# Weight slices of 512 columns for features 4 to 11, and an earlier issue for features 2 and 3, in an attention and feed-forward kernel

## Chip, cores and metric

One core of one Trainium2 chip. The time is the device time of one execution in microseconds (us), as the median of several executions; executions of one kernel mostly agree within about 1 us here. A profiled execution gives the trace from which all durations are read.

## What is computed

Linear attention followed by a gated feed-forward block, on 8,192 tokens (8 batches of 1,024) with 512 channels and 1,536 hidden columns:

```
k_proj, v_proj = E @ k, F @ v                 # per batch and head, 1024 rows -> 64
x      = softmax(q @ k_proj^T / 8) @ v_proj   # 8 heads of 64
g      = x @ w_gate ;  val = x @ w_val        # 512 x 1536 each
out    = (g * sigmoid(g) * val) @ w_out       # 1536 x 512
```

Inputs and weights are float32 in HBM. GpSimd's DMAs convert what they load to bf16 on the way in.

## The kernel before

The 1,536 hidden columns are 12 *features* of 128 columns. Tokens come in 16 chunks of 512. For every chunk and feature TensorE runs four matmuls for the gate and four for the value. The gate and value weights are loaded once, during the first 40 us, in slices of columns, and each slice is one DMA with one completion. All loads below are issued by GpSimd, in program order, between its normalisations (`u_N`).

```python
    def load_w_gv(c0, c1, which=(0, 1)):          # features c0 to c1-1; gate, then value
        cs = slice(c0 * P, c1 * P)
        for wsrc, wdst in [((moe_w_gate, wg), (moe_w_val, wv))[i] for i in which]:
            nc.gpsimd.dma_start(
                out=wdst[:, :, cs],
                in_=wsrc[:, cs].rearrange("(t p) c -> p t c", p=P),
            )
    ...
        load_q(0, 0, (0, 2))
        load_k(0, 4, 8)
        load_q(0, 0, (2, 4))
        load_v(0, (0, 4, 6, 8))
        load_w_gv(0, 1)
        load_w_gv(1, 2, (0,))
        ...
        u_N(0, 0)                                 # the first normalised unit
        load_w_gv(1, 2, (1,))
        ...
        u_N(0, 2)
        ...
        u_N(0, 1)
        load_w_gv(2, 4)
        ...
        load_w_gv(4, 6)
        load_q(0, 1)
        for f in (6, 8, 10):
            load_w_gv(f, f + 2)
        load_wo(0); load_wo(1); load_k(1)
        ...                                       # then chunk after chunk:
            f_g(c, f, i)                          # four gate matmuls, tanh on ScalarE
            run_slot(2 * t)                       # transposes of the next chunk's q, ...
            f_v(c, f, i)                          # four value matmuls, products on VectorE
```

The softmax here doesn't subtract the row's maximum and nothing guards it: scores larger than these inputs give would overflow.

## Time and profile before

| | before |
|---|---|
| time at the prediction | 573.21 us (573.05 to 573.64, 3 runs) |
| span of the profiled execution | 571.7 us |
| TensorE busy | 564.2 us |
| waits of TensorE for wg or wv | feature 6: 0.61 us (gate) + 0.29 us (value) |
| everything after feature 4 of the second chunk | 516.1 us |

"Busy" is time in which an engine executes; TensorE's 99% leaves little to win anywhere. Its timeline is the view that counts: in the columns start, duration, engine, line, operation, count, a bracket tells how long the engine was idle before and who ended it. The lines of before are in the prediction.

### The profile page before, as it was taken

Reading aid. Unit: us, or ns where it says so; the run is one execution under the profiler, and the core shown is the slowest. Engines: PE = TensorE matmul, PEld = TensorE weight load, DVE = VectorE, ACT = ScalarE, POOL = GpSimd, SP = SyncE. Lnnn points to the kernel's source line nnn. Section 1 sums busy time; section 2 is a strip of 40 time slices with the busy share of each in tenths; the row PEclk is TensorE's granted clock in tenths of the full one; section 3 lists DMA queues with packets and bytes.
Section 4 is the critical chain, followed back from the end, with each engine's and each line's share of the span. In section 5 each row is a group of like instructions: output and inputs, shape, how many; then the busy total and the mean of one; then the engine's idle time right before and its main releaser. Section 6 shows DMA issues by size and latency. Waiting matters only on the chain.

```text
span 571.7 us, 7944 instructions
## 1 busy us (share of the span) xinstructions
PE 564.2 (99%) x2971; PEld 268.5 (47%) x2971; DVE 336.6 (59%) x581; ACT 238.3 (42%) x421; POOL 109.2 (19%) x122
## 2 busy tenths in 40 slices
PE   8999999999999999999999999999999999999997
PEld 4644444444444444444444444444444444444444
DVE  3677566666466654666556665567546674554540
ACT  3555434354435434444335434354342543443232
POOL 6834121134002500124001330023200220000000
PEclk9999999999999999999999999999999999999999
DMA  9999993549901697038940499204990124100012
GB/s 202 176 199 206 202 177 77 89 71 197 202 29 47 113 192 148 19 75 129 196 100 37 64 176 196 63 20 90 196 176 37 44 50 75 38 37 23 33 38 92
DMA packets 106983, 61.86 MB, mean 108 GB/s; under 512 B 60096, under 2 KB 98240, under 8 KB 106944
## 3 DMA queue, kind: packets, MB, share of 16 engines
q0 software_dynamic: 42800, 29.36, 35.7%
q1 hardware_dynamic: 63232, 30.42, 24.7%
q10 hardware_dynamic: 912, 1.57, 1.0%
q8 instruction: 23, 0.38, 0.3%
q14 instruction: 16, 0.13, 0.1%
HBM read 60.29 MB, written 16.78 MB: 135 GB/s over the span
## 4 chain that ended last, share of the span: by engine, by line
PE 92%; DMA 3%; DVE 2%; POOL 1%; ACT 1%; issue 0%; DVEq 0%; POOLq 0%
PE yps L362 29%; PE vps L324 27%; PE gps L324 27%; PE kvp L149 3%; PE sc L229 2%; PE pv L287 2%; DMA wv<-in_moe_w_val_dram 2%; DMA qb<-in_q_dram 1%; DVE zz L244 1%; POOL AA L260 0%; POOL wg L117 0%; PE qTp L195 0%; DVE hT L348 0%; ACT xT L137 0%; DVE s L343 0%
## 5 line engine op out<-in xcount | busy, mean ns | idle before, releaser
L343 DVE SCALAR_TENSOR_TENSOR s<-th,gps 128x512 f32<-128x512 f32 x192 | 130.5, 680 | 139.2 <-ACT th L336 138.8
L324 PE MATMUL gps<-xT,wg 128*128 128x512 bf16 (+1 forms) x776 | 197.8, 377 | 0.7 <-DMA wg<-in_moe_w_gate_dram 0.4
L324 PE MATMUL vps<-xT,wv 128*128 128x512 bf16 (+1 forms) x776 | 197.5, 377 | 0.1
L362 PE MATMUL yps<-wo,hT 128*128 128x512 bf16 (+1 forms) x780 | 194.5, 376 | 0.0
L336 ACT ACTIVATE th<-gps 128x512 f32<-128x512 f32 x192 | 114.6, 597 | 163.4 <-PE gps L324 161.9
L348 DVE TENSOR_TENSOR hT<-s,vps 128x512 bf16<-128x512 f32 x192 | 132.0, 687 | 22.1 <-PE vps L324 1.5
L362 PEld LDWEIGHTS <-hT 128*128 128x128 bf16 x780 | 76.2, 98 | 89.9
L260 POOL TENSOR_TENSOR AAd<-ee,rr 128x512 bf16<-128x512 f32 x52 | 54.1, 1040 | 319.5 <-issue 178.1
L324 PEld LDWEIGHTS <-wv 128*128 128x128 bf16 x776 | 73.8, 98 | 83.2 <-issue 3.3
L324 PEld LDWEIGHTS <-wg 128*128 128x128 bf16 x776 | 74.0, 98 | 81.9 <-DMA wg<-in_moe_w_gate_dram 0.9
L372 ACT ACTIVATE ysb<-yps 128x512 f32<-128x512 f32 (+1 forms) x65 | 38.4, 590 | 78.1 <-PE yps L362 78.1
L137 ACT CAST xT<-pv 128x512 bf16<-128x512 f32 x63 | 36.7, 584 | 51.2 <-PE pv L287 50.3
L244 DVE TENSOR_REDUCE zz<-ee 128x8 f32<-128x512 f32 x64 | 43.5, 679 | 19.4 <-ACT ee L233 19.4
L233 ACT ACTIVATE ee<-sc 128x512 f32<-128x512 f32 x64 | 37.9, 596 | 18.0 <-PE sc L229 17.9
L287 PE MATMUL pv<-AT,BDV 128*128 128x512 bf16 x60 | 22.6, 379 | 0.0
L229 PEld LDWEIGHTS <-qTd 128*128 128x128 bf16 x208 | 16.0, 98 | 12.3
L229 PE MATMUL sc<-BD,qTd 128*128 128x128 bf16 x208 | 20.1, 219 | 0.0
L137 DVE CAST BDV<-kvp 64x256 bf16<-64x256 f32 x14 | 6.0, 427 | 22.1 <-ACT ks L159 19.1
L260 POOL TENSOR_TENSOR AA<-ee,rr 128x512 bf16<-128x512 f32 x11 | 11.4, 1038 | 36.3 <-DVE rr L246 34.4
L246 DVE RECIPROCAL rr<-zz 128x8 f32<-128x8 f32 x64 | 13.0, 203 | 6.7 <-DVE zz L244 0.5
L149 PE MATMUL kvp<-vb,FT 128*64 128x512 bf16 (+2 forms) x80 | 15.7, 339 | 0.3 <-ACT BDV L137 0.3
L149 PE MATMUL kvp<-kb,ET 128*64 128x512 bf16 (+1 forms) x72 | 15.5, 358 | 0.3 <-DVE kb L137 0.2
(51 smaller groups left out, 146.4 us busy)
## 6 DMA issues: line engine op xcount, KB each, us to landing
out_dram<-ysb SPq DMA_DIRECT2D x63, 256.0 KB, 2.4
qb<-in_q_dram POOLq DMA_DIRECT2D x15, 512.0 KB, 16.9
kb<-in_k_dram POOLq DMA_DIRECT2D x7, 1024.0 KB, 11.3
vb<-in_v_dram POOLq DMA_DIRECT2D x7, 1024.0 KB, 14.0
wo<-in_moe_w_out_dram POOLq DMA_DIRECT2D x2, 768.0 KB, 15.3
wg<-in_moe_w_gate_dram POOLq DMA_DIRECT2D x5, 256.0 KB, 9.6
wv<-in_moe_w_val_dram POOLq DMA_DIRECT2D x5, 256.0 KB, 10.2
kraw<-in_k_dram ACTq DMA_DIRECT2D x2, 512.0 KB, 5.0
```

The source lines that it names most:

```text
L137: (nc.scalar.copy if eng is nc.scalar else eng.tensor_copy)(out=out, in_=in_)
L149: nc.tensor.matmul(out=t[lo : lo + 64, h0:h1].rearrange("p h d -> p (h d)"), lhsT=w[:, j, :], rhs=src[b][:, h0:h1, j, :], start=(j == 0), ...
L229: nc.tensor.matmul(out=ps[:, n, :], lhsT=t[:, n, :], rhs=BD[b % 2][:, 4 * g + n, :], start=True, stop=True)
L233: nc.scalar.activation(out=e[:].rearrange("p h j k -> p (h j k)"), in_=ps[:].rearrange("p a k -> p (a k)"), func=AF.Exp, scale=scale,)
L244: nc.vector.reduce_sum(out=z[:], in_=e[:], axis=AX.X)
L260: eng.tensor_tensor(out=a.rearrange("p j h k -> p h j k"), in0=ee.pop((b, u))[:], in1=rr.pop((b, u))[:].unsqueeze(3).to_broadcast([P, 4, 2 ...
L324: nc.tensor.matmul(out=ps[:, ts], lhsT=(wg, wv)[w][:, kt, f * P : (f + 1) * P], rhs=x[:, kt, ts], start=(kt == 0), stop=(kt == NKT - 1),)
L336: nc.scalar.activation(out=th[:], in_=ps[:], func=AF.Tanh, scale=0.5)
L343: nc.vector.scalar_tensor_tensor(out=s1[:], in0=th[:], scalar=1.0, in1=g[:], op0=ALU.add, op1=ALU.mult)
L348: nc.vector.tensor_tensor(out=hT[c][:, f, :], in0=s1[:], in1=ps[:], op=ALU.mult)
L362: nc.tensor.matmul(out=yy[c][:, cs], lhsT=hT[c][:, f, i * P : (i + 1) * P], rhs=wo[:, f, cs], start=(f == 0), stop=(f == NFT - 1),)
L372: nc.scalar.activation(out=ysb[:, cs], in_=yy[c][:, cs], func=AF.Copy, scale=0.5)
```

## The change

Intent: use an idle stretch of GpSimd for the transfers of features 2 and 3, and move later weights in fewer, wider slices.

```diff
         u_N(0, 0)
         load_w_gv(1, 2, (1,))
+        load_w_gv(2, 4)
         ...
         u_N(0, 1)
-        load_w_gv(2, 4)
         ...
-        load_w_gv(4, 6)
+        load_w_gv(4, 8)
         load_q(0, 1)
-        for f in (6, 8, 10):
-            load_w_gv(f, f + 2)
+        load_w_gv(8, 12)
```

## The prediction

> **What bounds the kernel now.** I read the page first, then the waits of TensorE, then its timeline around the longest real wait, then GpSimd's timeline and the DMA issues one at a time.
>
> ```profile
> span 571.7 us, 7944 instructions
> PE 564.2 (99%) x2971; PEld 268.5 (47%) x2971; DVE 336.6 (59%) x581; ACT 238.3 (42%) x421; POOL 109.2 (19%) x122
> ...
> PE 92%; DMA 3%; DVE 2%; POOL 1%; ACT 1%; issue 0%; DVEq 0%; POOLq 0%
> PE yps L362 29%; PE vps L324 27%; PE gps L324 27%; PE kvp L149 3%; PE sc L229 2%; PE pv L287 2%; DMA wv<-in_moe_w_val_dram 2%; DMA qb<-in_q_dram 1%; DVE zz L244 1%; POOL AA L260 0%; POOL wg L117 0%; PE qTp L195 0%; DVE hT L348 0%; ACT xT L137 0%; DVE s L343 0%
> ```
>
> The first two lines cap everything: TensorE is busy 564.2 of 571.7 us, so a change that leaves its instructions alone has 7.5 us to play with, start and end of the program included. The chain says where a load still counts: its only weight entry is one transfer of wv, 2% of the span (10.19 us at 23.88 in time order). That is a path, not a gain; the gain is the idle time at its end. The timeline of TensorE there (start, duration, engine, line, operation, count, idle before and who ended it):
>
> ```profile
> 28.68 1.03 PE L324 MATMUL gps<-xT,wg 128*128 128x512 bf16 x4
> 29.55 1.03 PE L324 MATMUL vps<-xT,wv 128*128 128x512 bf16 x4
> 30.41 1.03 PE L324 MATMUL gps<-xT,wg 128*128 128x512 bf16 x4
> 31.27 1.03 PE L324 MATMUL vps<-xT,wv 128*128 128x512 bf16 x4
> 32.74 1.04 PE L324 MATMUL gps<-xT,wg 128*128 128x512 bf16 x4 [0.44 <-DMA wg<-in_moe_w_gate_dram]
> 33.61 0.39 PE L195 MATMUL qTp<-ident_bf,qb 128*128 128x128 bf16 x4
> 34.12 1.04 PE L324 MATMUL vps<-xT,wv 128*128 128x512 bf16 x4
> ```
>
> Groups of four follow each other every 0.86 us. Counting features from the head, 28.68 is feature 4 (gate), 29.55 its value, 30.41 and 31.27 feature 5, 32.74 and 34.12 feature 6. Feature 6 should have begun at 31.27 + 0.86 = 32.13: it is 0.61 late. Its value group should have followed at 32.74 + 0.87 + 0.22 (the four transposes) = 33.83: 0.29 late. Together 0.90 us of waiting for weights, and I find no other wait of this size for wg or wv anywhere in the run.
>
> GpSimd issues these loads, in its order:
>
> ```profile
> 13.59 1.04 POOL L260 TENSOR_TENSOR AA<-ee,rr 128x512 bf16<-128x512 f32 x1 [2.69 <-DVE rr L246]
> 14.58 0.80 POOL L117 DMA_DIRECT2D wv<-in_moe_w_val_dram  x1
> 17.28 2.04 POOL L260 TENSOR_TENSOR AA<-ee,rr 128x512 bf16<-128x512 f32 x2 [1.89 <-ACT ee L233]
> 19.27 0.80 POOL L117 DMA_DIRECT2D wg<-in_moe_w_gate_dram  x1
> 20.07 0.75 POOL L117 DMA_DIRECT2D wv<-in_moe_w_val_dram  x1
> ```
>
> It idles 1.89 us from 15.38 to 17.28, behind two normalisations that wait for ScalarE and VectorE, and only then issues features 2 and 3. Asked one by one, the issues land at (issue start + time to landing): value of feature 1, 14.58 + 8.0 = 22.6; gate 2-3, 19.27 + 4.7 = 23.9; value 2-3, 20.07 + 5.2 = 25.3; gate 4-5, 20.80 + 6.4 = 27.2; value 4-5, 21.53 + 7.0 = 28.5; q, 22.27 + 9.1 = 31.4; gate 6-7, 23.14 + 9.55 = 32.7; value 6-7, 23.88 + 10.19 = 34.1. The last two are exactly the two late groups. So until 34 us the weights are in a race with TensorE, and the queue is never empty. What it moves, by stretch (busy time of PE, PEld, DVE, ACT, POOL; clock, DMA share, GB/s):
>
> ```profile
> 21.00:22.00 1.00, 1.00 (x13) 0.88 (x11) 0.78 (x2) 0.28 (x1) 1.00 (x2) 1.00 1.34 131
> 22.00:23.00 1.00, 1.00 (x11) 0.90 (x10) 0.25 (x1) 0.58 (x1) 1.00 (x2) 1.00 1.34 170
> 23.00:24.00 1.00, 1.00 (x12) 0.89 (x10) 0.00 (x0) 0.14 (x1) 1.00 (x3) 1.00 1.46 191
> 24.00:25.00 1.00, 1.00 (x11) 0.88 (x9) 0.51 (x1) 0.72 (x2) 1.00 (x2) 1.00 1.15 128
> ...
> 30.00:31.00 1.00, 1.00 (x6) 0.47 (x5) 0.76 (x2) 0.34 (x1) 0.00 (x0) 1.00 1.46 196
> 40.00:41.00 1.00, 1.00 (x9) 0.50 (x6) 0.65 (x2) 0.60 (x1) 0.77 (x2) 1.00 1.26 210
> ```
>
> Steady rates are 196 (512-byte rows, at 30 us) and 210 (1,024-byte rows of w_out, at 40 us), but at 21 to 22 it moved only 131 and at 24 to 25 only 128: some 1 us of transfer was lost just before the late weights.
>
> **What the Trainium skill says.** "DMA: Bandwidth & Descriptors", section "Queues, rings and completion order": on each DMA engine descriptors are consumed in ring order. The landings above come in issue order, so I treat the queue as a line. Same page, "Why a DMA increments its semaphore by 16 and not by 1": only the full 16 means that all data has landed. So a wider slice releases its first feature only when its last has arrived; the trace of before has no weight slice of that width to show it. Same page, "Rules for kernel authors": coalesce transfers into large ones. The trace supports it mildly: 512 KB of v (1,024-byte rows) took 2.54 us of the queue (landings 13.6 and 16.1), while two 256 KB weight slices took 1.33 each later on: 5% better, no more. The page's fixed cost of about 2 us per transfer is not visible here between queued transfers.
>
> **The change part by part.** The listings of both builds differ only on GpSimd; TensorE, VectorE, ScalarE and SyncE keep every instruction in place (buffer numbers aside).
>
> (1) Features 2 and 3 issued in the idle 1.89 us. Each issue waits for the transfer eight places earlier (the listing's eight completion semaphores). For gate 2-3 that is the second half of q, landed 3.57 + 10.0 = 13.6: it issues at 15.38. For value 2-3 it is the first half of v, landed 4.44 + 11.7 = 16.1; after such a wait GpSimd restarts about 0.3 us later (9.9 to 10.16 in the trace), so 16.4 to 17.2. The normalisation at 17.28 just stays where it is; even 0.2 us later its readers on TensorE would still have slack, since the transposes begin at 18.72 and 19.61 while the results are ready at 18.3 and 19.3. Cost 0. Benefit: two transfers sit behind feature 1's before its end, which should fill part of the hole at 21 to 23. The hole against 196 is 65 + 26 KB, about 0.45 us. I count 0.3 of it, because the landing counts the slowest of 16 engines.
>
> (2) For features 4 to 11 eight slices of 256 KB become four of 512 KB. Four issues of about 0.8 us vanish from GpSimd: 3.2 us of an engine that is 19% busy and not on the path. Worth 0 by themselves. Rows double to 1,024 bytes: about 0.24 us per megabyte (2 x (2.66 - 2.54)), and I hope that the second hole (128 at 24 to 25) does not return, another 0.4.
>
> (3) The order of arrival changes, and this is the cost. Value of feature 4 used to need gate 4-5 and value 4-5: 28.5 against a use at 29.55, 1 us of slack. Now it needs gate 4-7 and value 4-7, 1 MB instead of 0.5. From value 2-3 at 25.3 - 0.3 = 25.0, two times 2.54 gives 30.1; with no hole at all and the slowest engine 1.0 us less behind (my guess, not read from a view) it would be 22.6 - 1.0 + 2.66 + 5.08 = 29.3. I take 29.9: a wait of 29.9 + 0.05 - 29.55 = 0.4 us at the value of feature 4 that was not there before.
>
> (4) Behind that, nothing waits at feature 6 (its weights are there): -0.90. q for the second half lands 2.8 later, 32.7, needed at about 33.0 + 0.4: fits. Gate 8-11 then lands at 35.2, needed at 36.9 + 0.4; value 8-11 at 37.8, needed at 38.0 + 0.4: slack 0.6, but tight. I charge 0.1.
>
> Sum: -0.90 + 0.4 + 0.1 = -0.4 us. 573.21 - 0.4 = 572.8.
>
> **The rivals.** A: the wide slices come in time (value 4-7 by 29.5). Then all 0.90 is kept: 572.3. For it: both holes of the DMA queue are before this point, and the issue is 4 us earlier. B: the slowest engine, not the queue, sets the landings; then gate 2-3 still lands at 23.9 and value 4-7 at 25.3 + 5.1 = 30.4, waits of 0.9 at feature 4 and some 0.2 at feature 8 eat it all: 573.3. For it: gate 2-3 landed 1.34 after feature 1's value, already the steady spacing. C: the normalisations slip behind the early issue, because the first half of v lands late. Every us there is a us of TensorE near 18.7 to 21. Against it: 0.3 us of margin on the results. It would make 573.5 to 574.
>
> **Range and chances.** Everything outside 15 to 45 us is the same instructions, so the rivals span 572.3 to 573.5; the three times of before spread 0.6 us by themselves. Range 572.2 to 573.6. A change of 2% is 11.5 us, more than all idle time of TensorE: 0.01 each way.
>
> **What would show it.** Right: TensorE's timeline without a wait at feature 6, a wait of 0.1 to 0.8 for wv at the value group near 29.5, GpSimd issuing at about 15.4 and 16.4 with the normalisations still at 17.3, and 21 to 22 us moving more than 131 GB/s. Wrong: gate 2-3 landing no earlier than 23.9 (rival B), no wait at feature 4 (rival A), or the normalisation later than 17.5 with waits on AA (rival C).

## The result, and the profile after

| | before | after |
|---|---|---|
| time, same rounds | 573.17 us (573.05 to 573.64, 4 runs) | 573.11 us (572.79 to 573.39, 4 runs) |
| ratio | | 0.9997, 95% interval 0.998 to 1.0015 |
| span of the profiled execution | 571.7 us | 571.6 us |

Ratios are the mean time of one kernel's runs over that of the other's of the same rounds, so they are not quite the ratio of the medians. The result is no change. But the trace did change. First lines of the page of the changed kernel:

```profile
span 571.6 us, 7940 instructions
...
PE 564.8 (99%) x2971; PEld 268.3 (47%) x2971; DVE 336.8 (59%) x581; ACT 238.2 (42%) x421; POOL 106.2 (19%) x118
```

Four instructions and 3.0 us are gone from GpSimd, as they should be, and nothing came of it. TensorE's timeline of the changed kernel, around features 4 to 6:

```profile
28.67 1.03 PE L324 MATMUL gps<-xT,wg 128*128 128x512 bf16 x4
30.37 1.04 PE L324 MATMUL vps<-xT,wv 128*128 128x512 bf16 x4 [0.67 <-DMA wv<-in_moe_w_val_dram]
31.25 1.03 PE L324 MATMUL gps<-xT,wg 128*128 128x512 bf16 x4
32.11 1.03 PE L324 MATMUL vps<-xT,wv 128*128 128x512 bf16 x4
32.97 1.03 PE L324 MATMUL gps<-xT,wg 128*128 128x512 bf16 x4
```

Before, features 4 and 5 ran without a gap and feature 6 came 0.61 and 0.29 late. After, feature 6 follows at once (32.11 + 0.86 = 32.97), but the value of feature 4 starts at 30.37 instead of 28.67 + 0.87 = 29.54: 0.83 late. A wait of 0.90 was exchanged for one of 0.83. (The bracket says 0.67, because the modelled end of the matmuls before it reaches into the gap. Starts are the safer measure.)

GpSimd of the changed kernel, and what its DMA queue moved (the columns are as in the prediction, GB/s last):

```profile
15.37 0.75 POOL L117 DMA_DIRECT2D wg<-in_moe_w_gate_dram  x1
16.41 0.74 POOL L117 DMA_DIRECT2D wv<-in_moe_w_val_dram  x1 [0.30 <-DMA vb<-in_v_dram]
17.26 2.04 POOL L260 TENSOR_TENSOR AA<-ee,rr 128x512 bf16<-128x512 f32 x2
```

```profile
21.00:22.00 1.00, 1.00 (x13) 0.88 (x10) 0.79 (x2) 0.26 (x1) 0.69 (x1) 1.00 1.54 194
22.00:23.00 1.00, 1.00 (x12) 0.89 (x11) 0.23 (x1) 0.58 (x1) 0.97 (x2) 1.00 1.46 196
24.00:25.00 1.00, 1.00 (x11) 0.86 (x9) 0.52 (x1) 0.72 (x2) 1.00 (x2) 1.00 1.24 205
```

The early issue worked as planned: features 2 and 3 leave at 15.37 and 16.41, the normalisations still start at 17.26, and the holes of the queue are closed (131 became 194 GB/s, 128 became 205). The question is why closed holes and a wait removed gave nothing.

For the first hole, at 21 to 23 us, the answer lies in when a DMA is complete. Each DMA is spread over 16 engines, and the trace records the completion of each share. The first, the fifteenth and the last of the 16, in us:

```
                       before                    after
value of feature 1     21.18   21.65   22.60     21.14   21.64   22.57
gate 2-3               22.92   23.76   23.94     22.49   22.97   23.91
value 2-3              24.29   25.09   25.30     23.83   24.31   25.28
gate 4-5 / gate 4-7    25.82   26.93   27.19     26.37   26.88   27.79
value 4-5 / value 4-7  27.52   28.27   28.54     28.91   29.39   30.33
```

Fifteen engines deliver features 2 and 3 up to 0.8 us earlier than before. The sixteenth delivers at the same time, 0.03 us earlier. It is about 1 us behind the others. In the kernel before the others came back to it by gate 2-3, because they stood in the hole; after the change nobody stands, and it stays behind. (The trace counts shares and does not name the engine. That the late share is always the same engine's is inferred: in both kernels the last shares of feature 1, gate 2-3 and value 2-3 come 1.34 to 1.37 us apart, the steady spacing, so one engine went on without a break.) TensorE waits for the last share: 30.33 for value 4-7, where the fifteenth was there at 29.39. By that share the slice would have been in time for its use at 29.54; no run was made without the lag.

The second hole, at 24 to 25 us, is another matter. Before, the last shares of value 2-3 and gate 4-5 are 1.89 us apart (25.30 and 27.19), so the slowest engine stood in this one too. Closing it does bring the later weights forward, as e1 shows; in the changed kernel the wider slice takes that gain away again, as e2 and e8 show.

### The profile page after: what moved, and what is told of

Its sections match the earlier page's. It is cut to its first block, busy times and chain, and to the rows that moved or that the text cites. A ratio compares the mean times of both kernels' runs of the same rounds, so it can differ in the third digit from the quotient of the medians.

```text
span 571.6 us, 7940 instructions
## 1 busy us (share of the span) xinstructions
PE 564.8 (99%) x2971; PEld 268.3 (47%) x2971; DVE 336.8 (59%) x581; ACT 238.2 (42%) x421; POOL 106.2 (19%) x118
## 4 chain that ended last, share of the span: by engine, by line
PE 92%; DMA 4%; DVE 1%; POOL 1%; ACT 1%; issue 0%; DVEq 0%; POOLq 0%
PE yps L362 29%; PE vps L324 28%; PE gps L324 28%; PE kvp L149 3%; PE sc L229 2%; PE pv L287 2%; DMA vb<-in_v_dram 2%; DMA wv<-in_moe_w_val_dram 2%; DVE zz L244 0%; DVE hT L348 0%; ACT xT L137 0%; POOL qb L107 0%; DVE s L343 0%; POOL AA L260 0%; PE kTp L174 0%
```

## The experiments

All kernels computed the right result. The diffs of the experiments are against the changed kernel; e7 is that kernel unaltered, e8 is e2 unaltered. Beside each kernel, runs of before were taken; the 10 of them on this chip had a median of 573.69 us (572.98 to 573.91).

To compare single profiles I cut every span at the same ScalarE instructions (the tanh of a feature), because the start of the program varies by some tenths from execution to execution. Length of each piece, in us; the last is everything from feature 4 of the second chunk to the end:

```
                       start to f2   f2 to f5   f5 to f10   f10 to f16   rest
before                    26.29        5.18       11.55        12.52     516.13
after                     26.28        6.03       10.64        12.53     516.13
e1 early only             25.93        5.18       10.81        12.53     516.20
e2 wide only              27.97        7.06       10.80        12.38     516.12
e3 split q                26.07        5.18       10.64        12.52     516.13
e4 late wide              25.95        5.18       11.70        12.38     516.19
e5 one slice of 8         26.76       12.45       11.43        12.52     516.14
e6 fetch earlier          26.29        5.39       10.64        12.53     516.12
e7 after again            26.65        6.00       10.64        12.51     516.13
e8 wide only again        26.62        7.09       10.64        12.53     516.15
```

Without any wait for weights the second piece is 5.18 and the third 10.64. The rest is the same within 0.08 in every kernel: nothing is won or lost later.

### e1: the early issue without the wide slices

```diff
-        load_w_gv(4, 8)
+        load_w_gv(4, 6)
         load_q(0, 1)
-        load_w_gv(8, 12)
+        for f in (6, 8, 10):
+            load_w_gv(f, f + 2)
```

> Features 2 and 3 issued early, all slices left at 256 columns. Theory (the time is set by when the slowest of the 16 DMA engines delivers; the early issue closes the holes of the queue, and the wide slice is what gave the gain back): value 2-3 lands at 25.3 as in both kernels so far, then 1.33 us a slice: gate 4-5 26.6, value 4-5 28.0, q 30.6, gate 6-7 32.0, value 6-7 33.3. No wait at feature 4, a wait of 0.0 to 0.2 in all at feature 6 instead of 0.90. Time 0.7 to 0.9 below before, about 572.4 us. Rival (early issue is worth nothing, because the queue is full anyway): feature 6 still waits 0.9 and the time equals before, 573.2.

Measured: 572.47 us (572.24 to 572.85, 5 runs), ratio 0.9983 (0.9971 to 0.9996). TensorE of this kernel around feature 6:

```profile
31.78 1.03 PE L324 MATMUL gps<-xT,wg 128*128 128x512 bf16 x4
32.64 0.39 PE L195 MATMUL qTp<-ident_bf,qb 128*128 128x128 bf16 x4
33.02 1.04 PE L324 MATMUL vps<-xT,wv 128*128 128x512 bf16 x4
```

The gate follows at once, the value is 33.02 - 32.64 - 0.22 = 0.16 late. Of 0.90 us of waiting 0.74 is gone, and no wait appears at feature 4. The early issue is worth the better part of the gain that the change as a whole did not show; the rival is out. The 0.74 is found again in the landings: from the last share of value 2-3 to that of gate 6-7 it took 7.39 us before (25.30 to 32.69) and 6.65 here (25.01 to 31.66), and 0.60 of the difference lies at the second hole, between value 2-3 and gate 4-5.

### e2 and e8: the wide slices without the early issue

```diff
-        load_w_gv(2, 4)          # the early one
         ...
         u_N(0, 1)
+        load_w_gv(2, 4)
```

> 512-column slices, features 2 and 3 left behind the normalisations. Theory: value 2-3 lands at 25.3, the hole at 24 to 25 us of before is there again, value 4-7 lands at 25.3 + 5.1 + 0 to 0.5 = 30.4 to 30.9, a wait of 0.85 to 1.4 at the value of feature 4, none at feature 6. Time 573.1 to 573.8, at or above before. Rival (the early issue brought nothing, the width alone moved the wait): the same 0.83 as in the changed kernel and the same time, 573.1.

Measured: 574.72 us (574.04 to 576.11, 5 runs), ratio 1.0026. This missed the expected 573.1 to 573.8. The profiled execution was the one of 576.11 us, and its first piece was 1.7 us longer than before's. E landed some 0.8 us late there, and after the wait of 1.70 us for it TensorE's granted clock (1.00 is full speed) was 0.50 from 7.63 to 11.04 us, which is part of the rest. Two of the five executions, 576.11 and 575.58 us, have a mean clock of 0.997; the other three took 574.04 to 574.72. So I ran it once more.

> The wide-only kernel unaltered, because its profiled execution had a late start (E landed 0.8 us later than in the others) and its five times spread over 2 us. Theory: with a start like that of the others, value 4-7 lands at 30.9 to 31.5 and the value of feature 4 waits 1.4 to 1.9: 0.5 to 1.0 us above before. Rival (the first measurement was a slow chip or a slow start and no more): equal to before and to the changed kernel within 0.3.

Measured: 574.56 us (574.27 to 574.80, 4 runs), ratio 1.0018 (1.0004 to 1.0032). TensorE of this second run, gate and value of feature 4:

```profile
29.21 1.04 PE L324 MATMUL gps<-xT,wg 128*128 128x512 bf16 x4
31.77 1.04 PE L324 MATMUL vps<-xT,wv 128*128 128x512 bf16 x4 [1.52 <-DMA wv<-in_moe_w_val_dram]
```

The value is 31.77 - 29.21 - 0.87 = 1.69 late, the gate another 0.19. 1.88 - 0.90 = 0.98 us lost against before, and the ratio says 1.0. Width alone is a loss. The early issue wins back about as much of it (e8 to e7 below: 574.56 to 573.37), and within the noise that is the whole of the change.

### e3: every piece placed by when it is needed

```diff
-        load_w_gv(4, 8)
-        load_q(0, 1)
-        load_w_gv(8, 12)
+        load_w_gv(4, 8, (0,))            # gate 4 to 7, wide
+        load_w_gv(4, 6, (1,))            # value 4 and 5
+        load_q(0, 1, (0, 2))
+        load_w_gv(6, 8, (1,))            # value 6 and 7
+        load_q(0, 1, (2, 4))
+        load_w_gv(8, 10)
+        load_w_gv(10, 12)
```

> Early issue kept; gate 4-7 wide, then value 4-5, the first half of q, value 6-7, the second half of q, then narrow slices for 8 to 11: each piece placed by the time at which TensorE needs it. Theory: gate 4-7 lands at 27.8, value 4-5 29.15, first half of q 30.7, value 6-7 32.0, second half of q 33.5; needed at 28.7, 29.5, 33.0, 33.2 and 34.1. No wait for weights or q from feature 2 on. Time 0.9 below before, 572.3. Rival (the waits are not the path, another wait takes their place): waits gone, time not below 573.

Measured: 572.32 us (572.24 to 572.92, 5 runs), ratio 0.9984 (0.997 to 0.9997). TensorE of this kernel, gate and value of feature 4:

```profile
28.46 1.03 PE L324 MATMUL gps<-xT,wg 128*128 128x512 bf16 x4
29.32 1.03 PE L324 MATMUL vps<-xT,wv 128*128 128x512 bf16 x4
```

Both pieces with waits are at their floor, 5.18 and 10.64: all 0.90 us of waiting is gone, and the time follows. This kernel and e1 beat both kernels of the case by about 0.9 us, or 0.16%; between them the runs don't decide. A wide slice is harmless where all of it lands before its first use: gate 4-7 was complete at 27.50 here and used from 28.46.

### e4: the wide slices for features 8 to 11 alone

```diff
-        load_w_gv(4, 8)
+        load_w_gv(4, 6)
         load_q(0, 1)
+        load_w_gv(6, 8)
         load_w_gv(8, 12)
```

> As the first of these runs, but 512 columns for features 8 to 11 alone. Theory: no wait at features 4 and 6 (0.0 to 0.2); gate 8-11 lands at 35.8, value 8-11 at 38.3 to 38.8 against a need at 38.1: a wait of 0.2 to 0.7 at the value of feature 8, which no kernel had so far. Time 572.6 to 573.1. Rival (width late in the queue is free): as the first run, 572.4.

Measured: 573.21 us (572.86 to 573.61, 5 runs), ratio 0.9994 (0.9981 to 1.0006); the time is just above the expected 572.6 to 573.1. TensorE at the value of feature 8, and the issue of value 8-11 with its time to landing:

```profile
37.57 0.39 PE L229 MATMUL sc<-BD,qT 128*128 128x128 bf16 x4
38.72 1.04 PE L324 MATMUL vps<-xT,wv 128*128 128x512 bf16 x4 [0.77 <-DVE zz L244]
```

```profile
wv<-in_moe_w_val_dram POOLq DMA_DIRECT2D x1, 512.0 KB, 14.8
```

It starts 38.72 - 37.57 - 0.22 = 0.93 late, more than the 0.2 to 0.7 expected: a second share was late by then (14 shares landed by 37.14, the fifteenth at 38.03, the last at 38.67; e6 tells the likely cause), and the start of this execution was 0.34 us early. The bracket names VectorE. That is an example of a wrong releaser: the slice was issued at 23.89 and landed 14.8 later, at 38.7, which is the moment at which TensorE goes on. With 0.11 at the value of feature 6 this kernel waits 1.04 us against 0.90 before, and its time equals before within the interval. In the changed kernel the same slice cost nothing, because its wait at feature 4 had already pushed feature 8 back.

### e5: the suspected cost doubled

```diff
-        load_w_gv(4, 8)
+        load_w_gv(4, 12)
         load_q(0, 1)
-        load_w_gv(8, 12)
```

> Early issue kept, features 4 to 11 as one slice of 1,024 columns for the gate and one for the value, then q. Doubles the suspected cost. Theory (a slice serves nothing until its last column has landed on the slowest DMA engine): gate 4-11 lands at 25.3 + 5.1 = 30.4, value 4-11 at 35.5; gate of feature 4 waits 1.7, its value another 4.2, then nothing waits. 5.9 us of waiting against 0.9 of before: time 578.2, 5.0 above before. Rival (TensorE needs only the columns it reads, or waits absorb each other later): within 1 us of before.

Measured: 580.76 us (579.80 to 581.47, 4 runs), ratio 1.0123. The direction is right, the size too small by 2 us. TensorE of this kernel, and two stretches:

```profile
28.29 1.03 PE L324 MATMUL vps<-xT,wv 128*128 128x512 bf16 x4
30.63 1.04 PE L324 MATMUL gps<-xT,wg 128*128 128x512 bf16 x4 [1.32 <-DVE hT L348]
35.58 1.89 PE L324 MATMUL vps<-xT,wv 128*128 128x512 bf16 x4 [3.91 <-DMA wv<-in_moe_w_val_dram]
37.26 1.91 PE L324 MATMUL gps<-xT,wg 128*128 128x512 bf16 x4
38.97 1.86 PE L324 MATMUL vps<-xT,wv 128*128 128x512 bf16 x4
40.67 1.03 PE L324 MATMUL gps<-xT,wg 128*128 128x512 bf16 x4
```

```profile
32.00:33.00 1.00, 0.00 (x0) 0.00 (x0) 0.67 (x1) 0.30 (x1) 0.00 (x0) 1.00 1.11 211
34.00:35.00 1.00, 0.00 (x0) 0.00 (x0) 0.00 (x0) 0.00 (x0) 0.00 (x0) 0.50 1.37 194
```

The waits are 30.63 - 28.29 - 0.87 = 1.47 at the gate and 35.58 - 30.63 - 0.87 = 4.08 at the value: 5.55 in all, near the 5.9 expected. The rest is the clock. While TensorE stood, its granted clock (the third number from the end) fell from 1.00 to 0.50, and the next three groups took about 1.7 us each instead of 0.86: 2.5 us more. 5.55 + 2.5 - 0.9 = 7.15, and the medians differ by 7.07. The Trainium skill, "TensorE: Matmul & The Clock Gate", Part 1, says that the array's clock is halved after an idle window of about 3.4 us. The halving is as it says, but the idle time is not: here the clock fell at 33.82, 2.15 us after the last matmul had ended (31.67, a modelled end), and in e2's profile it fell at 7.63, after a wait of 1.70 us and 0.7 us after TensorE had begun to work again. No run shows the shortest wait that does it.

### e6: the instruction fetch moved

The lag of the sixteenth engine needs a cause. Near its beginning the trace has one packet of 16,384 bytes on the queue named "instruction" (19.71 us in the changed kernel, taking 0.945 us). The Trainium skill, "Runtime: NRT & Kernel Launch", section "Instruction fetch mechanics", says that an engine's instructions are refilled by DMA in blocks of 16 KiB, which are 256 instructions. The trace agrees: by 19.71 us TensorE had executed 250 matmuls and weight loads of the program, more than any other engine. To test that this fetch is the lag, I gave TensorE more instructions at its start, with the same number of streamed columns (the cut leaves out that `warm` was given a width as its second argument):

```diff
-        warm(11)            # 11 warming matmuls of 512 columns
+        warm(44, P)         # 44 of 128 columns
```

> The changed kernel with its first 11 warming matmuls of 512 columns made into 44 of 128 (same streamed columns, 66 more TensorE instructions before everything else). Theory (one DMA engine is 1 us late because it carried a 16 KB instruction fetch at 19.7 us, which comes when TensorE has gone through some 250 instructions): the fetch comes at about 16.3 us instead, and the engine's lag shows 3 us earlier: the second and third piece of v land at 18.2 to 18.5 and 19.4 to 19.7 instead of 17.4 and 18.7, gate of feature 0 at 20.2 to 20.4 instead of 19.4. Value 4-7 still lands at 30.3, so the time is that of the changed kernel within 0.4. Rival (the lag belongs to the slices of features 0 and 1 or to that time): the second and third piece of v and gate 0 land as before, value 0 is the first to be late.

Measured: 572.76 us (572.63 to 572.77, 4 runs), ratio 0.9986 (0.9973 to 1.0). The packet came at 15.21 us, when TensorE had executed 240 (240 to 252 in all ten traces), and the lag moved with it. Fifteenth and last share, in us:

```
                        after              e6
first piece of v        16.12   16.13      15.55   15.62
second piece of v       17.42   17.44      16.93   17.71
third piece of v        18.66   18.68      18.17   19.00
gate of feature 0       19.40   19.42      18.91   19.73
value of feature 0      20.17   21.75      19.65   20.50
value 4-7               29.39   30.33      28.88   29.70
```

In the changed kernel the last share falls behind at the value of feature 0. Here it falls behind at the second piece of v, three transfers earlier, and stays 0.8 us behind until value 4-7. So the fetch is the cause; the rival is out. The other traces fit: in all ten, the first transfer with a late last share lands right after the packet. In e7, which is the changed kernel unaltered, the packet came at 20.25, just before value 0 landed at 20.52, and it is gate 1 that lags first (21.30 and 22.37). A second packet, at 36.60 in the changed kernel and at 36.62 in e4, comes just before the second late share, at value 8-11. TensorE now feels the lag at v:

```profile
17.76 0.63 PE L149 MATMUL kvp<-vb,FT 128*64 128x128 bf16 x8 [1.02 <-DMA vb<-in_v_dram]
```

My expectation missed two things. The landings moved less than I wrote, because the whole queue ran some 0.5 us earlier in this execution (first piece of v: 15.62 against 16.13). And the wait at feature 4 became 5.39 - 5.18 = 0.21 us instead of about 0.83, so that this kernel came out about 0.6 us better than the changed one (573.37 below), where I expected 0.4 at most. The wait for v held TensorE back by about what the queue was ahead (the first piece is 26.29, as before), so TensorE met the same feature with the weights closer. Whether all four executions started that way, one profile doesn't tell.

### e7: the changed kernel again

> The changed kernel unaltered, beside before on the same chip with five rounds. Theory: 0.83 us of waiting at feature 4 in place of 0.90 at feature 6: within 0.3 us of before. Rival (the change is worth some tenths that four runs hid): 0.4 us or more below before.

Measured: 573.37 us (572.68 to 573.71, 6 runs), ratio 0.9995 (0.9983 to 1.0008). Its trace has 6.00 - 5.18 = 0.82 us of waiting before feature 5 and none at feature 6. The change is worth nothing, and its two halves are worth about plus and minus one microsecond.

## Why the prediction was right, and where it was off

- **What bounds the kernel, and that only 15 to 45 us could change.** Right: the rest is 516.13 us before and after, and the first piece differs by 0.01.
- **Step 1, the early issue is free and fills holes.** The issues fell at 15.37 and 16.41 (predicted 15.38 and 16.4), the normalisations stayed. But I counted 0.3 us of the first hole for the landing of features 2 and 3, "because the landing counts the slowest of 16 engines"; that reason should have led to 0. It was 0.02 to 0.03 (23.91 and 25.28 against 23.94 and 25.30). My guess that the slowest engine would be 1.0 us less behind had nothing behind it, and averaging with it gave the 29.9.
- **Step 2, fewer instructions and the second hole.** Right: 3.0 us less of GpSimd gave nothing, and the stretch at 24 us moved 205 GB/s.
- **Step 3, the wide slice moves the wait to feature 4.** The mechanism was right, its size was the mis-sized term: value 4-7 landed at 30.33, not 29.9, and the wait was 0.83, not 0.4. Rival B of the prediction (gate 2-3 still at 23.9, value 4-7 at 30.4) is what happened, but for its wait of 0.2 at feature 8. By its own signs, then, the main account was wrong: gate 2-3 landed at 23.91, not earlier than 23.9, and the wait was outside the 0.1 to 0.8 that it named. The figure that should have decided was in its own text: gate 2-3 came 1.34 after feature 1's value, already the steady spacing.
- **Step 4, feature 6 and what lies behind it.** The 0.90 came back in full (third piece 11.55 to 10.64). q was there. The 0.1 charged at feature 8 did not fall due: value 8-11 landed at 38.65, and its group started on time at 38.85. e4 shows how near that was.
- **The sum.** -0.90 + 0.83 = -0.07 us in place of -0.4; the measured medians differ by 0.06. The time fell into the range because the range was made to hold rival B, and not because the sum was right.

Open: why the queue had its holes before. The first begins with the late issue of features 2 and 3. The second, at 24 to 25 us, comes with slices that had been issued 3 us earlier, and it returned in e8, where features 2 and 3 are late as well (160 and 164 GB/s at 24 to 26 us there, against 205 and 210 after; gate 4-7 landed 2.8 to 3.6 us behind value 2-3 there, against 2.5 after). It goes away with the early issue, but no run shows by which mechanism.

## What to carry to other kernels

A slice that is loaded as one DMA serves nothing until its last byte is there, so while loads race with the engine that uses them, cut them by when they are needed and make them wide only where there is slack. Read a transfer's landing from its slowest share: here, closing a gap in the queue helped only where the engine that finishes last was standing in it. When a change with two parts shows nothing, run each part alone before calling both worthless.

## What the Trainium skill lacked or had wrong

- "Runtime: NRT & Kernel Launch", section "Instruction fetch mechanics", calls the cost of crossing a 16 KiB block "mostly hidden". That speaks of the engine whose instructions are fetched; for the data in a full queue beside it the cost was not hidden: one fetch of 0.945 us put one of 16 DMA engines 0.8 to 1.0 us behind, and every later DMA of that queue completed that much later, for over 10 us (29.39 against 30.33).
- "DMA: Bandwidth & Descriptors", section "Rules for kernel authors", advises to coalesce transfers and does not say that the completion of a wide transfer comes later for its first columns: slices of 512 instead of 256 columns cost 0.98 us here (e8), slices of 1,024 columns 7.1 us (e5), of which 2.5 are the halved clock. What coalescing gave back was 5% of the transfer time (2.54 us for 512 KB, as between gate 4-7 and value 4-7 after the change, against 2 x 1.33).
- The same page has no word on the catching up of a lagging DMA engine. It kept its lag of about 0.95 us over 8 us of a full queue, and lost it while the queue moved 131 and 170 GB/s instead of 196 (0.95 to 0.18 us between the value of feature 1 and gate 2-3 of before).
- "TensorE: Matmul & The Clock Gate", Part 1, has an idle window of about 3.4 us before the clock is halved. Here it was halved after waits that were shorter by then: 2.15 us in e5, and 1.70 us in e2.
